# A cheaper VectorE exponential in 96 bursts, the skip product on VectorE, and a second state bank laid out by quarters, in a fused SSM and attention kernel

## The chip, the cores and the metric

One core of one Trainium2 chip. The metric is device time in microseconds (us), the median of several executions. Every experiment ran beside the kernel before on the same chip. Different batches of experiments ran on different chips, so the ratios to the kernel before compare across batches better than the bare times do.

## The reference, cut to what matters

Two branches on one input of 2048 rows and 1024 columns, mixed row by row by a gate.

```python
g = sigmoid((x * gate_w).sum(-1, keepdims=True))
a = A_ref(x, ...)     # SSM: h = Lam_bar*h + Bu over 2048 steps; y = 2*Re(C h) + x*Dskip
b = B_ref(x, ...)     # attention: 32 heads of 32 columns; softmax(q k^T / sqrt(32)) v; then @ wo
return g * a + (1 - g) * b
```

The attention has 32 x 2048 x 2048 exponentials. They decide the time.

## The kernel before

Attention runs as 512 *bursts* in 8 groups of 64 (a group is four heads). A burst makes the scores of four heads, 256 queries and 256 keys in PSUM (the memory that TensorE writes its results to), and two 128x1024 exponentials turn them into bf16 weights. All instruction orders are static. The projections of the next group, the SSM's input products ("u"), its C chains ("c") and the output products fill TensorE's gaps; VectorE evicts them, which means that it copies them out of PSUM, and does the SSM's scans.

In some bursts (the list `DVB`) VectorE does half of one of the two exponentials, so that ScalarE has 512 columns less to do there. VectorE's half needs tiles: two for weights (`xt`), one for bits (`xi`) and one for scratch (`xw`). There are five sets of these, cut from memory that is idle at that time. Sets 0 and 1 lie in the weight buffers of the projections, but their scratch is a separate tile, `Ag[:, 1]`, which both share.

```python
self.xt = half(wx[0]) + half(wx[1]) + half(hx[0]) + half(self.OT[:, 6, :]) + [ub[:, 0], ub[:, 1]]
self.xw = [ag, ag, hx[1][:, 1024:2048].bitcast(F32), self.OT[:, 7, 1024:2048].bitcast(F32), self.ut[:, 1, :]]
# ... cut ...
def x_set(self, B):
    g, pg = divmod(B, 64)
    if g == 7 or B >= 433:
        return 4
    if pg < 52:                      # first 52 bursts of a group: the group's old weight buffer
        return g % 2
    return 2 if g < 4 else 3         # the last 12: other memory, with a scratch of its own

def x_toks(self, k):                 # what a load over set k claims to write
    # ... cut: asserts ...
    return [(n, t0 + t) for n in ("pt", "ptd") for t in range(2)] + [("xi", k), ("xw", max(k, 1))]
```

Every dependency goes through such *tokens*: an operation waits for the last writer of what it reads, and for the last writer and all readers of what it claims to write. `("xw", 1)` stands for the scratch of sets 0 and 1. At burst 58 of a group the weights of the next group but one are loaded over the old buffer. These are three loads of 256 KB on SyncE's queue:

```python
def ld_w(self, g, part, eng="sp"):
    cb = 1024 * part + 128 * g
    self.dma(lambda e: e.dma_start(self.w[:, g % 2, part], self.wsrc[:, :, cb:cb + 128]), [],
             [("w", g % 2, part)] + (self.x_toks(g % 2) if g > 2 else []), "ld_w", eng)
# ... cut ...
            if pg == (58 if g else 24) and g + 2 < GROUPS:
                for part in (1, 2, 0):
                    self.ld_w(g + 2, part)
```

VectorE's half exponential has five steps, dribbled between other VectorE work during the bursts after its own:

```python
self.S.op("dve", ... tensor_scalar(xi, ps[:, 2 * s + 1, :], EXP_A, EXP_B, ALU.mult, ALU.add) ...)          # exp_a, at once
self.dx += [(0.365, ... tensor_scalar(hi, hi, 0.0, 128.0, ALU.max, ALU.mult), [I], [I], "exp_b"),
            (0.603, ... scalar_tensor_tensor(xw, lo, EXP_C2, lo, ALU.add, ALU.mult), [I], [W], "exp_c"),     # W = ("xw", max(k, 1))
            (0.603, ... scalar_tensor_tensor(xw, xw, EXP_C1, lo, ALU.add, ALU.mult), [I, W], [W], "exp_d"),
            (0.603, ... scalar_tensor_tensor(t[:, 1, :], xw, EXP_C0, ev, ALU.add, ALU.mult), [I, W], [("ptd", p)], "exp_f")]
```

## Time and profile before

| | |
|---|---|
| time | 929.05 us (928.53 to 929.23, 4 runs) |
| profiled span, mean granted TensorE clock | 926.5 us, 0.998 |
| bursts with a half exponential on VectorE | 82 |
| ScalarE: spacing of the ends of consecutive operations, median | 0.917 us (1024 columns), 0.490 us (512) |
| ScalarE's floor, 942 x 0.917 + 84 x 0.490 | 905 us |

The spacings come from the trace's records, since durations of overlapping operations say nothing of throughput.

The page of the kernel before (busy time and share; then busy tenths of a fortieth of the span each):

```profile
PE 892.4 (96%) x15095; PEld 525.4 (57%) x15316; DVE 737.3 (80%) x1331; ACT 911.3 (98%) x1034; POOL 8.9 (1%) x39
...
ACT  6999999999999999999999999999999999999997
...
PE 55%; ACT 37%; DVE 5%; issue 1%; SPq 1%; DMA 1%; DVEq 0%
...
L1666 ACT ACTIVATE f_pt<-f_ps 128x1024 bf16<-128x1024 f32 x862 | 814.2, 1209 | 0.6 <-PE f_ps L1650 0.6
```

Windows of the kernel before (busy us and instructions of TensorE, its weight loads, VectorE, ScalarE and GpSimd in this order; then granted clock, DMA share, GB/s):

```profile
200.00:300.00 100.00, 98.10 (x1622) 56.35 (x1643) 89.78 (x159) 100.00 (x114) 0.00 (x0) 1.00 0.22 49
300.00:400.00 100.00, 98.29 (x1702) 58.39 (x1724) 85.26 (x155) 99.96 (x116) 1.41 (x6) 1.00 0.20 46
```

ScalarE is never idle between its start and its end: the large group of exponentials shows 0.6 us of idle time before it in the whole run. TensorE holds more of the chain of waits, but its weight loads (PEld) stand idle for ScalarE's exponentials, so it follows ScalarE, and ScalarE is what bounds. In the list of waits (us in total, times, longest):

```profile
PEld f_ps L1650 <- ACT f_pt L1666: 63.4, 153, 0.6
```

### The profile page before, as it was taken

How to read it: one execution, taken by the hardware profiler on the slowest of the kernel's cores; microseconds unless marked ns; L12 is line 12 of the kernel's file. 1: busy time of each engine (PE TensorE's matmuls, PEld its weight loads, DVE VectorE, ACT ScalarE, POOL GpSimd, SP SyncE). 2: the span in 40 equal slices, each digit the busy share in tenths (PEclk: the TensorE clock that was granted, in tenths of full speed). 3: DMA queues.
4: the chain of work that ended last, by engine and by line, in shares of the span. 5: the costliest groups of instructions: out<-in, count | busy, mean ns of one | idle time of the engine just before them, and what ended most of it. 6: DMA issues, size and time to landing. Idle time of an engine off the chain costs nothing.

```text
span 926.5 us, 33493 instructions
## 1 busy us (share of the span) xinstructions
PE 892.4 (96%) x15095; PEld 525.4 (57%) x15316; DVE 737.3 (80%) x1331; ACT 911.3 (98%) x1034; POOL 8.9 (1%) x39
## 2 busy tenths in 40 slices
PE   8899999999999999999999999999999999999996
PEld 4555755566555655555755755555565655555553
DVE  2799999999888888867889966679888765766775
ACT  6999999999999999999999999999999999999997
POOL 2000000000000000000000000000000000000000
PEclk9999999999999999999999999999999999999999
DMA  9649613210230113113033102133210111434322
GB/s 202 107 79 156 106 31 74 42 42 28 66 72 30 30 43 73 41 40 53 19 75 58 25 16 65 53 66 59 39 38 12 52 52 56 161 88 122 117 65 75
DMA packets 157076, 60.90 MB, mean 66 GB/s; under 512 B 145664, under 2 KB 145664, under 8 KB 156928
## 3 DMA queue, kind: packets, MB, share of 16 engines
q1 hardware_dynamic: 154768, 58.16, 28.3%
q8 instruction: 121, 1.98, 0.9%
q10 hardware_dynamic: 2160, 0.53, 0.3%
q14 instruction: 27, 0.22, 0.1%
HBM read 16.79 MB, written 12.58 MB: 32 GB/s over the span
## 4 chain that ended last, share of the span: by engine, by line
PE 55%; ACT 37%; DVE 5%; issue 1%; SPq 1%; DMA 1%; DVEq 0%
ACT f_pt L1666 33%; PE f_ps L1725 16%; PE f_ps L1650 11%; PE f_ps L1480 8%; PE f_ps L1451 8%; PE f_ps L1421 8%; PE f_ps L1439 4%; SPq L1074 1%; ACT f_ub L1691 1%; ACT f_wb L1691 1%; DVE f_ht L1370 1%; DMA f_xT<-in_A_x_dram 1%; ACT f_Et L1666 1%; ACT f_cT_re L1666 1%; PE f_ps L1486 1%
## 5 line engine op out<-in xcount | busy, mean ns | idle before, releaser
L1666 ACT ACTIVATE f_pt<-f_ps 128x1024 bf16<-128x1024 f32 x862 | 814.2, 1209 | 0.6 <-PE f_ps L1650 0.6
L1725 PEld LDWEIGHTS f_ps<-f_V,f_pt 128*128 128x128 bf16 x6896 | 239.4, 96 | 135.9 <-issue 96.9
L1725 PE MATMUL f_ps<-f_V,f_pt 128*128 128x33 bf16 x6896 | 293.0, 178 | 0.2 <-ACT f_pt L1666 0.2
L1650 PE MATMUL f_ps<-f_Q,f_K 32*128 32x256 bf16 x4096 | 220.9, 273 | 4.2 <-ACT f_pt L1666 1.2
L1650 PEld LDWEIGHTS f_ps<-f_Q,f_K 32*128 32x128 bf16 x4096 | 72.7, 92 | 118.4 <-ACT f_pt L1666 63.4
L1451 PE MATMUL f_ps<-f_xT,f_wb 128*128 128x512 bf16 x448 | 117.4, 377 | 8.2 <-issue 2.1
L1421 PE MATMUL f_ps<-f_xT,f_wb 128*128 128x512 bf16 x406 | 106.7, 378 | 4.5 <-issue 0.5
L1370 DVE TENSOR_TENSOR_SCAN f_ht<-f_pf,f_init,f_ut 128x512 bf16<-128x512 f32 x64 | 80.2, 1271 | 0.0
L1692 DVE TENSOR_SCALAR f_wb<-f_ps 128x512 int32<-128x512 f32 x53 | 36.6, 691 | 52.4 <-PE f_ps L1650 52.3
L1480 PE MATMUL f_ps<-f_cT_im,f_hp 128*128 128x512 bf16 x189 | 71.4, 378 | 3.0
L1511 PE MATMUL f_ps<-f_wb,f_OT 128*128 128x512 bf16 x218 | 57.8, 378 | 3.0 <-issue 0.2
L1451 PEld LDWEIGHTS f_ps<-f_xT,f_wb 128*128 128x128 bf16 x512 | 40.2, 96 | 33.4 <-issue 1.9
L1439 PE MATMUL f_ps<-f_wb,f_xT 128*128 128x128 bf16 x896 | 59.1, 219 | 0.0
L1480 PE MATMUL f_ps<-f_cT_re,f_hp 128*128 128x512 bf16 x147 | 55.5, 378 | 0.2
L1421 PEld LDWEIGHTS f_ps<-f_xT,f_wb 128*128 128x128 bf16 x464 | 36.2, 96 | 28.2 <-DVE f_ub L1457 0.3
L1439 PEld LDWEIGHTS f_ps<-f_wb,f_xT 128*128 128x128 bf16 x896 | 50.4, 97 | 0.0
L1457 DVE CAST f_ub<-f_ps 128x512 bf16<-128x512 f32 x48 | 33.0, 687 | 14.5 <-PE f_ps L1451 14.1
L1362 DVE TENSOR_TENSOR f_tq<-f_ht,f_Et 128x1024 bf16<-128x1024 bf16 x64 | 42.3, 684 | 0.4
L1362 DVE TENSOR_TENSOR f_ut<-f_tq 128x512 f32<-128x512 bf16 x64 | 42.3, 683 | 0.0
L1691 ACT ACTIVATE f_wb<-f_ps 128x512 bf16<-128x512 f32 x53 | 38.4, 725 | 0.1
L1701 DVE SCALAR_TENSOR_TENSOR f_wb<-f_Ag,f_wb 128x512 bf16<-128x512 f32 x53 | 36.5, 689 | 1.2
L1700 DVE SCALAR_TENSOR_TENSOR f_Ag<-f_Ag,f_wb 128x512 f32<-128x512 f32 x53 | 36.3, 685 | 0.7
(160 smaller groups left out, 925.4 us busy)
## 6 DMA issues: line engine op xcount, KB each, us to landing
ag_scratch<-f_Ag SPq DMA_DIRECT2D x32, 256.0 KB, 2.3
f_hp<-ag_scratch SPq DMA_DIRECT2D x32, 256.0 KB, 3.0
f_wb<-in_B_wqkv_dram SPq DMA_DIRECT2D x21, 256.0 KB, 3.5
out_dram<-f_xT SPq DMA_DIRECT2D x16, 256.0 KB, 2.1
f_wb<-in_B_wo_dram SPq DMA_DIRECT2D x1, 1024.0 KB, 6.2
f_OT<-f_On SPq DMA_TRANSPOSE x63, 2.4
f_wb<-in_B_wo_dram SPq DMA_DIRECT2D x1, 768.0 KB
f_wb<-in_B_wqkv_dram ACTq DMA_DIRECT2D x2, 256.0 KB, 4.1
```

The costliest lines, as they stand in the source:

```text
L1362: ops.append((c, lambda: dve(lambda e: e.tensor_tensor(o, a, b, op), r, w() if callable(w) else w)))
L1370: ops.append((1.192, lambda ri=ri: dve(lambda e: e.tensor_tensor_scan(ht[:, ri, :], rr, ut[:, ri, :], self.init[:, ri, j:j + 1], ALU.mult, ...
L1421: mms.append((1, lambda e, f, l, a=a: e.matmul(ps[:, bank, :], w[:, g % 2, part, a, :], xT[:, a, 512 * ch:512 * (ch + 1)], start=f, stop=l ...
L1439: m = e.matmul(ps[:, bank, 128 * q:128 * (q + 1)], xT[:, a, 128 * kt:128 * (kt + 1)], w[:, g % 2, 2, a, :], start=(a == 0), stop=(a == 7))
L1451: mms.append((1, lambda e, f, l, a=a: e.matmul(ps[:, 7, :], bT[:, n % 2, ri, a, :], xT[:, a, 512 * ch:512 * (ch + 1)], start=f, stop=l), [ ...
L1480: mms.append((1, lambda e, f, l, j=j, ri=ri: e.matmul(ps[:, 7, :], hp[:, ri, j, cols], cT[ri][:, j, 512 * cb:512 * (cb + 1)], start=f, sto ...
L1511: mms.append((1, lambda e, f, l, j=j: e.matmul(ps[:, 7, :], OT[:, j, 256 * qb + 128 * r:256 * qb + 128 * (r + 1)], wo[j][0][:, 512 * cb:51 ...
L1650: m = e.matmul(ps[:, 2 * sl[z] + h % 2, 256 * kl:256 * (kl + 1)], K[32 * h:32 * h + 32, g % 2, 128 * kt:128 * (kt + 1)], Q[32 * h:32 * h + ...
L1666: self.act(lambda e: e.activation(self.tile[p], ps[:, 2 * s:2 * s + 2, :], ACT.Exp, scale=SCALE), [("S", s)], [("pt", p)], "exp")
L1691: self.S.op("act", lambda e: e.activation(t[:, 0, :], ps[:, 2 * s, :], ACT.Exp, scale=SCALE), reads=[("S", s)], writes=[("pt", p)], deps=d ...
L1692: self.S.op("dve", lambda e: e.tensor_scalar(xi, ps[:, 2 * s + 1, :], EXP_A, EXP_B, ALU.mult, ALU.add), reads=[("S", s)], writes=[("xi", k ...
L1725: m = e.matmul(ps[:, 6, o:o + 33], self.tile[p][:, h2, 256 * kl + 128 * qt:256 * kl + 128 * (qt + 1)], V[:, g % 2, 2 * i + kl, h, :], star ...
```

## The change

Four intents:
- a four-step exponential on VectorE that leaves bf16 bits (Q scaled at its eviction, bias and scale in ScalarE's exponential);
- 96 bursts in place of 82;
- the product x * Dskip no longer as 128 diagonal matmuls in the C chains, but as 64 VectorE operations on x in rows, loaded by 64 small DMAs;
- the second bank of SSM states laid out by row quarters, so that it is freed quarter by quarter and its C chains can run late.

Sets 2 and 3 of the tiles go, since C chains now use that memory for longer. The lists `ORDER` and `DVB_RUNS` are new. The diff, cut to its core:

```diff
-        self.xw = [ag, ag, hx[1][:, 1024:2048].bitcast(F32), self.OT[:, 7, 1024:2048].bitcast(F32), self.ut[:, 1, :]]
+        self.xw = [ag, ag, self.ut[:, 1, :]]
 ... cut ...
+    def x_group(self, B):
+        g, pg = divmod(B, 64)
+        return g if pg < 54 else g + 1
+
     def x_set(self, B):
-        g, pg = divmod(B, 64)
-        if g == 7 or B >= 433:
-            return 4
-        if pg < 52:
-            return g % 2
-        return 2 if g < 4 else 3
+        return 2 if B >= 433 else self.x_group(B) % 2
 ... cut: exponential ...
-            self.act(... ACT.Exp, scale=SCALE) ...
+            self.act(... ACT.Exp, bias=OCTAVES * LN2, scale=LN2 / 128) ...
+        self.S.op("dve", ... tensor_scalar(xi, ps[:, 2 * s + 1, :], BITS_0, BITS_MIN, ALU.add, ALU.max) ... "exp_a")
+        self.dx += [(0.603, ... scalar_tensor_tensor(xw, lo, 65536.0, lo, ALU.subtract, ALU.mult), [I], [W], "exp_b"),
+                    (0.603, ... scalar_tensor_tensor(xw, lo, CUBE_C, xw, ALU.add, ALU.mult), [I, W], [W], "exp_c"),
+                    (0.603, ... scalar_tensor_tensor(bits, xw, CUBE_K, xi, ALU.mult, ALU.add), [I, W], [("ptd", p)], "exp_d"),
 ... cut: C chain ...
-        for q in range(4):
-            dt = 4 * cb + q
-            mms.insert(5 * q + 3, (0, ... matmul(... xT[:, dt, ...], self.diagD[:, dt, :], start=False, stop=False) ...))
+    def skip_ops(self, ch, tq, cb):          # two operations of 128x256 per C chain
+        ... scalar_tensor_tensor(self.Ag[:, 0, 256 * k:256 * (k + 1)], self.xn[k], self.gcol[:, 0, tt:tt + 1], self.drow[:, c0:c0 + 256], ALU.mult, ALU.mult) ...
         def evac():
+            self.dve(... scalar_tensor_tensor(a, ps[:, 7, :], self.gcol[:, 0, tt:tt + 1], a, ALU.mult, ALU.add) ... "evac_c")
             self.dma(lambda e: e.dma_start(self.agd[tile], a), ... "st_a")
+            if self.c_next < 32:
+                self.ld_xn(*self.c_list[self.c_next])     # two loads of x for the next chain, 64 KB each
```

More of the change, by code (lines that the diff above doesn't have):

```diff
@@ L24 @@
 G_MIN = 1e-30
-RC_MIN = 1e-10
-RC_MAX = 1e12
 class Op:
@@ L930 @@
 ACT_1 = 0.49
-ACT_LAG = 0.466
+ACT_LAG = 0.12
 QK_LAG = 0.449
@@ L938 @@
 DEP = 0.122
-EXP_A = 16713.9646930418
-EXP_B = 4936176.0
-EXP_C2 = 189883.03836007958
-EXP_C1 = 38303098318.667244
-EXP_C0 = 3607248267949745.0
+LOG2E = 1.4426950408889634
+Q_SCALE = 128.0 * LOG2E * SCALE
+OCTAVES = 65
+BITS_0 = 128.0 * (127 + OCTAVES)
+BITS_MIN = 16384.0
+CUBE_C = 3.891446932518378 * 65536.0
+CUBE_K = 0.07826797 * 128.0 / 65536.0 ** 3
+LN2 = 0.6931471805599453
+DEN_MIN = 1e-12 * 2.0 ** OCTAVES
+DEN_MAX = 1e10 * 2.0 ** OCTAVES
 ORDER = "".join(w[0] * int(w[1:]) for w in (
-    "u2 p2 u4 p1 u2 p2 u2 p9 u8 p1 u1 p1 u1 p1 u1 p1 u1 p1 u1 p1 u1 p1 c1 p2 c1 p2 c1 p1 u4 c1 u2 p1 c1 p2 c1 u2 p4 c1 p2 c1 u2 p3 u2 c2 u1 c6 u1 p12 u4 "
-    "p1 u2 p1 u4 p9 c5 p1 c3 u4 p1 u2 p1 u2 p1 u4 p1 u2 p8 u2 p9 c8 p3 o36 ").split())
-DVB_RUNS = ((109, 113), (129, 177), (185, 257), (277, 277), (285, 329), (345, 345), (365, 381), (389, 453), (461, 505))
+    "u2 p3 u1 p3 u1 p1 u4 p2 u2 p5 u3 p2 u2 p2 u1 p3 u1 p3 u1 p1 u5 p1 u1 c3 p8 u2 p2 c1 u3 c1 p1 u1 c1 u2 p1 c2 u2 p2 u2 p2 c2 p1 u2 p4 u2 p2 u2 c1 p1 c1 "
+    "u2 c1 p3 u2 p4 u2 p1 c2 p1 c1 p2 c2 p1 c3 p3 c3 u4 p2 u2 p1 u2 p1 u2 p2 u1 p3 u3 p3 u1 p2 u1 p4 c8 p3 o36 ").split())
+DVB_RUNS = ((65, 65), (70, 70), (73, 73), (84, 84), (114, 118), (121, 121), (129, 129), (134, 134), (137, 141), (150, 162), (165, 177), (182, 202), (205, 209), (214, 238), (241, 241), (246, 246), (249, 257), (262, 262), (265, 265), (270, 278), (281, 281), (286, 294), (297, 309), (314, 326), (329, 333), (340, 340), (346, 346), (358, 370), (373, 373), (381, 381), (386, 394), (402, 402), (405, 413), (418, 418), (421, 421), (426, 434), (437, 441), (446, 450), (453, 453), (459, 459), (462, 462), (465, 465), (470, 486), (489, 493), (498, 498), (501, 501), (508, 508))
 DVB = {B for lo, hi in DVB_RUNS for B in range(lo, hi + 1, 4)}
@@ L991, in __init__ @@
         self.Et = T("Et", [128, 2, 8, 512], BF)
-        hp = T("hp", [128, 2, 8, 512], BF)
-        self.hpb = [hp, self.OT[:, 4:8, :].rearrange("p (r a) n -> p r (a n)", r=2).rearrange("p r (j t) -> p r j t", j=8)]
+        hp = self.hp = T("hp", [128, 2, 8, 512], BF)
+        cols = self.OT[:, 4:8, :].rearrange("p q (r j t) -> p q r j t", r=2, j=8)
+        self.hp_out = [lambda r, j: hp[:, r, j, :].rearrange("p (q t) -> p q t", q=4), lambda r, j: cols[:, :, r, j, :]]
+        self.hp_in = [lambda q, r, j: hp[:, r, j, 128 * q:128 * (q + 1)], lambda q, r, j: cols[:, q, r, j, :]]
         self.hp_of = [0, 1, 0, 0]
@@ L1007, in __init__ @@
         self.ones = T("ones", [128, 128], BF)
-        self.diagD = T("diagD", [128, 8, 128], BF)
+        self.drow = T("drow", [128, 1024], BF)
+        xa = T("xa", [128, 256], BF)
         self.init = T("init", [128, 2, 8], F32)
@@ L1015, in __init__ @@
         self.badb = T("badb", [128, 2], BF)
+        self.xn = [xa[:], self.pf[:, 24:40, :].bitcast(BF).rearrange("p a b -> p (a b)")]
         otf = self.OT.bitcast(F32)
@@ L1030, in __init__ @@
         half = lambda ap: [pair(ap[:, 0:1024]), pair(ap[:, 1024:2048])]
-        hx = [hp[:, r, 4:8, :].rearrange("p a n -> p (a n)") for r in range(2)]
         wx = [self.w[:, x].rearrange("p q a n -> p (q a n)") for x in range(2)]
         ag = self.Ag[:, 1, :]
-        self.xt = half(wx[0]) + half(wx[1]) + half(hx[0]) + half(self.OT[:, 6, :]) + [ub[:, 0], ub[:, 1]]
-        self.xi = [wx[0][:, 2048:3072], wx[1][:, 2048:3072], hx[1][:, 0:1024], self.OT[:, 7, 0:1024], self.ut[:, 0, :]]
-        self.xi = [ap.bitcast(I32) for ap in self.xi]
-        self.xw = [ag, ag, hx[1][:, 1024:2048].bitcast(F32), self.OT[:, 7, 1024:2048].bitcast(F32), self.ut[:, 1, :]]
+        self.xt = half(wx[0]) + half(wx[1]) + [ub[:, 0], ub[:, 1]]
+        self.xi = [wx[0][:, 2048:3072], wx[1][:, 2048:3072], self.ut[:, 0, :]]
+        self.xi = [ap.bitcast(F32) for ap in self.xi]
+        self.xw = [ag, ag, self.ut[:, 1, :]]
         self.tile += self.xt
@@ L1096, in begin @@
         pool, dve, act = self.pool, self.dve, self.act
-        warm = self.hpb[0][:, 0, 0, :]
+        warm = self.hp[:, 0, 0, :]
         dve(lambda e: e.memset(warm, 0.0), [], ["warm"])
@@ L1165, in evac @@
             kw.update(dict(writes=[tok]) if first else dict(acc=[tok]))
-            if eng is dve:
+            if tok[0] == "K":
                 S.op("dve", lambda e: e.tensor_copy(dst, src), name="evac_qk", **kw)
+            elif eng is dve:
+                S.op("dve", lambda e: e.tensor_scalar(dst, src, Q_SCALE, None, ALU.mult), name="evac_qk", **kw)
             else:
-                S.op("act", lambda e: e.activation(dst, src, ACT.Copy), name="evac_qk", **kw)
+                S.op("act", lambda e: e.activation(dst, src, ACT.Copy, scale=Q_SCALE), name="evac_qk", **kw)
         for word in self.OPENING.split():
@@ L1222, in opening @@
                 self.nmath = len(self.bg2)
-                self.diag_d()
     def spare(self, us):
@@ L1308, in math, with ld_d, ld_xn @@
         return ops
-    def diag_d(self):
-        for j in range(8):
-            self.pool(lambda e, j=j: e.tensor_scalar(self.diagD[:, j, :], self.ident[:], self.pf[:, 3, j:j + 1], 0.0, ALU.mult, ALU.add),
-                      ["ident", ("pf", 3)], [("diagD", j)])
+    def ld_d(self):
+        self.dma(lambda e: e.dma_start(self.drow[:], self.d["A_Dskip"].partition_broadcast(128)), [], ["drow"], "ld_d")
+    def ld_xn(self, ch, tq, cb):
+        tt = 4 * ch + tq
+        for k in range(2):
+            over = ["iot", "ioth", "ioti", ("pw2", 0), ("pw2", 1)] if k and self.c_next == 0 else []
+            c0 = 512 * cb + 256 * k
+            self.dma(lambda e, k=k, c0=c0: e.dma_start(self.xn[k], self.x2[128 * tt:128 * (tt + 1), c0:c0 + 256]), [], [("xn", k)] + over, "ld_xn")
+        self.c_next += 1
+    def skip_ops(self, ch, tq, cb):
+        tt = 4 * ch + tq
+        ops = []
+        for k in range(2):
+            c0 = 512 * cb + 256 * k
+            ops.append((0.335, lambda k=k, c0=c0: self.dve(lambda e: e.scalar_tensor_tensor(self.Ag[:, 0, 256 * k:256 * (k + 1)], self.xn[k], self.gcol[:, 0, tt:tt + 1],
+                                                                                            self.drow[:, c0:c0 + 256], ALU.mult, ALU.mult),
+                                                           [("xn", k), "drow", "g0"], [("Ag", 0)] if k == 0 else [("Ag", 0, 1)], "skip")))
+        return ops
     def fold_ops(self, j):
@@ L1352, in item_ops @@
         b = self.hp_of[ch]
-        hp = self.hpb[b]
-        er, ei = self.Et[:, 0, j, :], self.Et[:, 1, j, :]
+        hp = self.hp_out[b]
         k = self.ub_of(n)
@@ L1358, in item_ops @@
         t = [tq[:, i, :] for i in range(4)]
+        t4 = [tq[:, i, :].rearrange("p (q t) -> p q t", q=4) for i in range(4)]
         ops = []
@@ L1376, in item_ops @@
         hw = ["warm"] if ch == 0 and j == 0 else []
-        late = lambda: []
-        if ch == 2 and j >= 4:
-            late = lambda: self.x_toks(2)
         if b == 1 and j == 0:
             hw = ["fX", "fY", "m_c"] + self.EFtok + ["gp%d" % i for i in range(4)]
-        tt(0.335, hp[:, 0, j, :], t[0], t[1], ALU.subtract, [("tq", 0)], lambda: [("hp", b, j, 0)] + hw + late())
-        tt(0.335, hp[:, 1, j, :], t[2], t[3], ALU.add, [("tq", 2)], lambda: [("hp", b, j, 1)] + hw + late())
+        tt(0.335, hp(0, j), t4[0], t4[1], ALU.subtract, [("tq", 0)], lambda: self.hp_toks(b, j, 0) + hw)
+        tt(0.335, hp(1, j), t4[2], t4[3], ALU.add, [("tq", 2)], lambda: self.hp_toks(b, j, 1) + hw)
         if j == 7 and ch < 3:
@@ L1386, in item_ops, with hp_toks, hp_all @@
         return ops
+    def hp_toks(self, b, j, ri):
+        return [("hp", b, j, ri, q) for q in range(4 if b else 1)]
+    def hp_all(self, b, qs=range(4)):
+        return [("hp", b, j, ri, q) for j in range(8) for ri in range(2) for q in (qs if b else (0,))]
     def carry(self):
@@ L1425, in d_qk @@
             dst, tok = self.Q[:, z, :], ("Q", z)
+            evac = lambda: self.dve(lambda e: e.tensor_scalar(dst, ps[:, bank, :], Q_SCALE, None, ALU.mult), [("bank", bank)], [tok], "evac_qk")
         else:
             dst, tok = self.K[:, g % 2, 512 * ch:512 * (ch + 1)], ("K", g % 2, ch)
-        return self.chain(mms, "proj", lambda: self.dve(lambda e: e.tensor_copy(dst, ps[:, bank, :]), [("bank", bank)], [tok], "evac_qk"), bank)
+            evac = lambda: self.dve(lambda e: e.tensor_copy(dst, ps[:, bank, :]), [("bank", bank)], [tok], "evac_qk")
+        return self.chain(mms, "proj", evac, bank)
     def d_v(self, g, f, bank=7):
@@ L1473, in d_c @@
         b = self.hp_of[ch]
-        hp = self.hpb[b]
+        hp = self.hp_in[b]
         tt = 4 * ch + tq
-        cols = slice(128 * tq, 128 * (tq + 1))
         mms = []
@@ L1479, in d_c @@
             for ri in range(2):
-                mms.append((1, lambda e, f, l, j=j, ri=ri: e.matmul(ps[:, 7, :], hp[:, ri, j, cols], cT[ri][:, j, 512 * cb:512 * (cb + 1)], start=f, stop=l),
-                            [("hp", b, j, ri), ("cTf", ri, j)]))
-        for q in range(4):
-            dt = 4 * cb + q
-            mms.insert(5 * q + 3, (0, lambda e, f, l, q=q, dt=dt: e.matmul(ps[:, 7, 128 * q:128 * (q + 1)], xT[:, dt, 128 * tt:128 * (tt + 1)], self.diagD[:, dt, :],
-                                                                          start=False, stop=False), [("diagD", dt)] + self.xtok(ch)))
+                mms.append((1, lambda e, f, l, j=j, ri=ri: e.matmul(ps[:, 7, :], hp(tq, ri, j), cT[ri][:, j, 512 * cb:512 * (cb + 1)], start=f, stop=l),
+                            [("hp", b, j, ri, tq if b else 0), ("cTf", ri, j)]))
         a = self.Ag[:, 0, :]
@@ L1492, in evac @@
         def evac():
-            self.dve(lambda e: e.tensor_scalar(a, ps[:, 7, :], self.gcol[:, 0, tt:tt + 1], None, ALU.mult), [("bank", 7), "g0"], [at], "evac_c")
-            self.dma(lambda e: e.dma_start(self.agd[tile], a), [at], [("agd", tile)], "st_a")
+            self.dve(lambda e: e.scalar_tensor_tensor(a, ps[:, 7, :], self.gcol[:, 0, tt:tt + 1], a, ALU.mult, ALU.add), [("bank", 7), "g0", ("Ag", 0, 1)], [at], "evac_c")
+            self.dma(lambda e: e.dma_start(self.agd[tile], a), [at, ("Ag", 0, 1)], [("agd", tile)], "st_a")
+            if self.c_next < 32:
+                self.ld_xn(*self.c_list[self.c_next])
             self.c_left[ch] -= 1
@@ L1501, in ld_a @@
         tile = self.a_order[k]
-        x = [("hp", 0, j, ri) for j in range(8) for ri in range(2)] if k == 0 else []
+        x = self.hp_all(0) if k == 0 else []
         self.dma(lambda e: e.dma_start(self.Al[k % 8], self.agd[tile]), [("agd", tile)], [("Al", k % 8)] + x, "ld_a")
@@ L1554, in plan @@
                 late = B in DVB and q == 1
-                parts.append((B + 2 + (2 if late else 0), B, q))
+                parts.append((max(B + 2, min(B + 4, NBURST - 1)) if late else B + 2, B, q))
         todo = [sorted(parts[32 * U:32 * U + 32]) for U in range(NBURST // BURSTS)]
@@ L1614, in split_pv @@
         return need + rest[:len(rest) - n], rest[len(rest) - n:]
+    def x_group(self, B):
+        g, pg = divmod(B, 64)
+        return g if pg < 54 else g + 1
     def x_set(self, B):
-        g, pg = divmod(B, 64)
-        if g == 7 or B >= 433:
-            return 4
-        if pg < 52:
-            return g % 2
-        return 2 if g < 4 else 3
+        return 2 if B >= 433 else self.x_group(B) % 2
     def x_of(self, B, n):
-        return len(self.tile) - 10 + 2 * self.x_set(B) + n
+        return len(self.tile) - 6 + 2 * self.x_set(B) + n
     def x_toks(self, k):
-        t0 = len(self.tile) - 10 + 2 * k
+        t0 = len(self.tile) - 6 + 2 * k
         assert not any(self.left_in.get(t0 + t, 0) for t in range(2)), (self.p, k)
@@ L1665, in exp @@
         else:
-            self.act(lambda e: e.activation(self.tile[p], ps[:, 2 * s:2 * s + 2, :], ACT.Exp, scale=SCALE), [("S", s)], [("pt", p)], "exp")
+            self.act(lambda e: e.activation(self.tile[p], ps[:, 2 * s:2 * s + 2, :], ACT.Exp, bias=OCTAVES * LN2, scale=LN2 / 128), [("S", s)], [("pt", p)], "exp")
     def dve_exp(self, B, s, p):
@@ L1671, in dve_exp @@
         xi, xw, t = self.xi[k], self.xw[k], self.tile[p]
-        halves = xi.bitcast(U16).rearrange("p (n two) -> p n two", two=2)
-        lo, hi = halves[:, :, 0], xi.bitcast(I16).rearrange("p (n two) -> p n two", two=2)[:, :, 1]
-        ev = xi.bitcast(BF).rearrange("p (n two) -> p n two", two=2)[:, :, 1]
+        lo = xi.bitcast(U16).rearrange("p (n two) -> p n two", two=2)[:, :, 0]
+        bits = t[:, 1, :].bitcast(I16)
         deps = []
-        use = (k, B // 64 if k < 2 else 0)
+        wg = self.x_group(B)
+        use = (k, wg if k < 2 else 0)
         self.x_now = k
@@ L1680, in dve_exp @@
             if k < 2:
-                assert self.busy_w != B // 64
+                assert self.busy_w != wg and not self.proj[wg]
                 over = [("w", k, q) for q in range(3)] + [("Ag", 1)]
-            elif k < 4:
-                assert self.c_left[k - 2] == 0
-                over = [("hp", k - 2, j, ri) for j in range(8) for ri in range(2)]
             else:
@@ L1690, in dve_exp @@
                 deps += [self.S.tok_w.get(o)] + self.S.tok_r.get(o, [])
-        self.S.op("act", lambda e: e.activation(t[:, 0, :], ps[:, 2 * s, :], ACT.Exp, scale=SCALE), reads=[("S", s)], writes=[("pt", p)], deps=deps, name="exp")
-        self.S.op("dve", lambda e: e.tensor_scalar(xi, ps[:, 2 * s + 1, :], EXP_A, EXP_B, ALU.mult, ALU.add), reads=[("S", s)], writes=[("xi", k)], deps=deps, name="exp_a")
+        self.flush_dx()
+        self.S.op("act", lambda e: e.activation(t[:, 0, :], ps[:, 2 * s, :], ACT.Exp, bias=OCTAVES * LN2, scale=LN2 / 128), reads=[("S", s)], writes=[("pt", p)], deps=deps, name="exp")
@@ L1693, in dve_exp @@
+        self.S.op("dve", lambda e: e.tensor_scalar(xi, ps[:, 2 * s + 1, :], BITS_0, BITS_MIN, ALU.add, ALU.max), reads=[("S", s)], writes=[("xi", k)], deps=deps, name="exp_a")
         kw = max(k, 1)
         I, W = ("xi", k), ("xw", kw)
-        assert not self.dx, (self.p, [c for c, _ in self.dx], self.log[-8:])
         self.waiting.add(B)
         self.last_dx, self.dx_due = True, B + 3
-        self.dx += [(0.365, lambda: self.dve(lambda e: e.tensor_scalar(hi, hi, 0.0, 128.0, ALU.max, ALU.mult), [I], [I], "exp_b")),
-                    (0.603, lambda: self.dve(lambda e: e.scalar_tensor_tensor(xw, lo, EXP_C2, lo, ALU.add, ALU.mult), [I], [W], "exp_c")),
-                    (0.603, lambda: self.dve(lambda e: e.scalar_tensor_tensor(xw, xw, EXP_C1, lo, ALU.add, ALU.mult), [I, W], [W], "exp_d")),
-                    (0.603, lambda: self.dve(lambda e: e.scalar_tensor_tensor(t[:, 1, :], xw, EXP_C0, ev, ALU.add, ALU.mult), [I, W], [("ptd", p)], "exp_f")),
-                    (0.0, lambda: self.waiting.discard(B))]
+        self.dx += [(0.603, lambda: self.dve(lambda e: e.scalar_tensor_tensor(xw, lo, 65536.0, lo, ALU.subtract, ALU.mult), [I], [W], "exp_b")),
+                    (0.603, lambda: self.dve(lambda e: e.scalar_tensor_tensor(xw, lo, CUBE_C, xw, ALU.add, ALU.mult), [I, W], [W], "exp_c")),
+                    (0.603, lambda: self.dve(lambda e: e.scalar_tensor_tensor(bits, xw, CUBE_K, xi, ALU.mult, ALU.add), [I, W], [("ptd", p)], "exp_d")),
+                    (0.0, lambda: self.done_dx(B))]
@@ new lines, in done_dx, with flush_dx, dx_ready @@
+    def done_dx(self, B):
+        self.waiting.discard(B)
+        self.dx_end[B] = self.dve_t
+    def flush_dx(self):
+        while self.dx:
+            c, f = self.dx.pop(0)
+            self.dve_t += c + DEP * (c > 0)
+            f()
+    def dx_ready(self, quarters):
+        todo = [B for B, q in quarters if B in DVB and q == 1]
+        if any(B in self.waiting for B in todo):
+            self.flush_dx()
+        return max([self.dx_end.get(B, 0) + 0.12 for B in todo], default=0.0)
@@ L1740, in normalize @@
                                                   accum_out=self.osum[:, U:U + 1]), ["O", ("rc", U)], [("On", U % 2), ("os", U)], "norm")
-        x = [("hp", 1, j, ri) for j in range(8) for ri in range(2)] if g >= 4 and qb == 0 else []
-        assert not x or self.c_left[1] == 0
+        x = self.hp_all(1, [g - 4]) if g >= 4 and qb == 0 else []
+        assert not x or self.c_left[1] <= 14 - 2 * g
         if g < 4 and qb == 0:
@@ L1747, in normalize @@
                 x += [("ub", k, ri) for k in (2, 3) for ri in range(2)]
-        if qb == 0 and g >= 6:
-            assert all(self.x_set(B) != 3 or B < U * BURSTS for B in DVB)
-            x += self.x_toks(3)
         self.dma(lambda e: e.dma_start_transpose(self.OT[:, g, 256 * qb:256 * (qb + 1)].rearrange("p (t q) -> p t q", t=2),
@@ L1785, in build @@
         proj[0] = [self.d_qk(0, 0, 2), self.d_qk(0, 0, 3)]
+        self.proj = proj
         us, cs = [], []
+        self.c_list, self.c_next, self.bgx = [], 0, []
         for ch in range(4):
@@ L1790, in build @@
                     us.append((ch, 8 * ch + j, ri, self.d_u(j, ch, 8 * ch + j, ri)))
-            for cb in range(2):
-                for tq in range(4):
+            for tq in range(4):
+                for cb in range(2):
                     cs.append((ch, self.d_c(ch, tq, cb, len(cs))))
+                    cs[-1][1].pre = lambda ch=ch, tq=tq, cb=cb: self.skip_ops(ch, tq, cb)
+                    self.c_list.append((ch, tq, cb))
         self.c_left = [8, 8, 8, 8]
@@ L1816, in build @@
         log = self.log = []
+        self.dx_end = {}
         for p in range(first, NBURST):
@@ L1828, in build @@
                 self.dve_t = max(self.dve_t, T + QK_LAG) + 0.608
-                ta = max(ta, self.dve_t + 0.19)
+                ta = max(ta, self.dve_t + 0.1)
             nq += len(self.quarters[p])
@@ L1835, in build @@
             head, tail = self.split_pv(p, ntail)
+            rdy = self.dx_ready(head)
             self.pv(head)
             second()
-            pe = T + QK_PE + PV_PE * len(head)
+            pe = max(T + QK_PE + PV_PE * len(head), rdy + PV_PE)
             if ends:
@@ L1852, in build @@
                 self.later.pop(0)[1]()
+            if not self.c_next and len(self.tabled) == 8:
+                self.ld_d()
+                self.ld_xn(*self.c_list[0])
             if pg == (58 if g else 24) and g + 2 < GROUPS:
@@ L1883, in build @@
                     kind = order[0]
+                    assert kind != "c" or not self.bgx
                     if kind == "p":
@@ L1897, in build, with take @@
                         ok = self.items_done >= 8 * (cs[0][0] + 1) and p > self.item_p + 1 and len(self.folded) == 8
-                        take = lambda: cs.pop(0)[1]
+                        def take():
+                            self.bgx, self.bgx_at = cs[0][1].pre(), p + 2
+                            return cs.pop(0)[1]
                     else:
@@ L1915, in build @@
                     quota += 1
+            rdy = self.dx_ready(tail)
             self.pv(tail)
             ready = pe + 0.2
+            pe = max(pe, rdy)
             tp = pe + PV_PE * len(tail) + 0.1
@@ L1931, in build @@
             if ended is not None:
+                while self.bgx:
+                    c, f = self.bgx.pop(0)
+                    f()
+                    self.dve_t += c
                 ended.evac()
@@ L1960, in sources @@
         out = []
-        for src in (self.bg, self.bg2):
-            if not src:
+        for src in (self.bgx, self.bg, self.bg2):
+            if not src or src is self.bgx and self.p < self.bgx_at:
                 continue
@@ L1979, in tail @@
         z = self.ut[:, 1, 0:65]
-        dve(lambda e: e.memset(z, 0.0), [], ["z"] + [("ut", r) for r in range(2)] + self.x_toks(4))
-        assert not self.dx, (self.p, [c for c, _ in self.dx], self.log[-8:])
+        dve(lambda e: e.memset(z, 0.0), [], ["z"] + [("ut", r) for r in range(2)] + self.x_toks(2))
         def check(u0, u1, s0, s1, c):
@@ L1987, in check @@
             rcs, oss = [("rc", u) for u in range(u0, u1)], [("os", u) for u in range(s0, s1)]
-            dve(lambda e: e.tensor_scalar(t, ra, RC_MAX, None, ALU.is_le), rcs, [("ut", 0)])
-            dve(lambda e: e.scalar_tensor_tensor(t, ra, RC_MIN, t, ALU.is_ge, ALU.mult, accum_out=chk[:, c:c + 1]), rcs + [("ut", 0)], [("ut", 0), ("chk", c)])
+            dve(lambda e: e.tensor_scalar(t, ra, 1.0 / DEN_MIN, None, ALU.is_le), rcs, [("ut", 0)])
+            dve(lambda e: e.scalar_tensor_tensor(t, ra, 1.0 / DEN_MAX, t, ALU.is_ge, ALU.mult, accum_out=chk[:, c:c + 1]), rcs + [("ut", 0)], [("ut", 0), ("chk", c)])
             dve(lambda e: e.scalar_tensor_tensor(z2, osum[:, s0:s1], 0.0, z[:, s0:s1], ALU.mult, ALU.is_equal, accum_out=chk[:, c + 1:c + 2]), oss + ["z"], ["z2", ("chk", c + 1)])
@@ L1996, in preload @@
                          reads=["ident", ("hi", 2 * r), ("lo", 2 * r)], name="preload", writes=[("tb", 2 + r)] + ([("S", 1)] if r == n == 0 else []), **({} if r == n == 0 else dict(acc=[("S", 1)])))
+        self.dx_ready([(NBURST - 2, 1), (NBURST - 1, 1)])
         check(0, 63, 0, 63, 0)
```

## The prediction

> **What bounds it now.** ScalarE. The page has it busy 98% of 926.5 us, the windows view 99.96 to 100 us of every 100 from 100 to 800 us. Its operations overlap, so I took the spacing of their ends in the trace: 0.917 us (median) for a 128x1024 exponential, 0.490 us for a 128x512 one. There are 942 of the first and 84 of the second (82 bursts give half of one exponential to VectorE): a floor of 942 x 0.917 + 84 x 0.49 = 905 us. By the timeline the first exponential starts at 9.7 us and the last ends at 918.0: 908.3 us, about 4 over the floor; then 8.5 us of tail. TensorE (96% busy) holds most of the chain of waits (55%, ScalarE 37%), but its weight loads wait some 75 us for exponentials (waits), so it follows ScalarE. VectorE is 80% busy, 94 to 96% from 50 to 200 us.
>
> **What the change does.**
> - ScalarE: the diff's lists hold 82 bursts before and 96 after. 14 more exponentials are halved: 14 x (0.917 - 0.490) = 6.0 us off the engine that bounds. The new bias should cost nothing: the Trainium skill ("ScalarE: Activation LUTs", "What ACT_TABLE_LOAD costs") gives 186 ns + 0.833 ns per element with immediate scale and bias, 93 ns more for a pointer operand. The trace agrees with the immediate form: shortest durations 1017 and 597 ns at 1024 and 512 elements.
> - VectorE: a burst's exponential goes from five operations (0.69 + 0.45 + 3 x 0.69 = 3.2 us by the groups) to four (2.75 us): 82 x 3.2 = 262 us becomes 96 x 2.75 = 264 us. The skip product adds 64 operations of 128x256 at some 0.4 us (an estimate from the 0.42 us of other 128x256 operations): +26 us. The eviction stays 0.75 us. VectorE's busy time rises from 737 to about 765 us, still below the 94 to 96% that the early stretches bear without costing ScalarE anything.
> - TensorE: 128 diagonal matmuls of 128x128 go; their busy 27.9 us overlaps, some 7 us of real time (estimate: a quarter of the 0.22 us pitch of 512-column matmuls each). Off the critical path; slack for the C chains.
> - Moves: C chains later, bursts spread more evenly (some from burst 65 on, more from 256 to 288), 64 small loads of x. Queue room is ample (mean 66 GB/s).
>
> **On the critical path:** the 6.0 us only; the rest makes room for it. I expect the excess over the floor to stay at 4 to 5 us. The profile's span should go from 926.5 to about 921.
>
> **Predicted: 923.5 us, 920.5 to 927.5 (8 in 10).** Faster by over 2%: 0.01; within 2%: 0.96; slower by over 2%: 0.03.
>
> **What would show it.** Right: ScalarE still at 99 to 100 us per 100; 928 full exponentials 0.917 us apart, 98 half ones, floor 899 us; VectorE 755 to 775 us busy; no diagonal matmuls; TensorE's share unchanged or a point down; head and tail unchanged. Wrong: gaps between exponentials behind a late first step of VectorE's exponential (QK weight loads waiting for VectorE), above all before 300 us.
>
> **What would make it wrong.** A bias taken from memory (93 ns on 1024 operations, up to +95 us); VectorE behind its static order, so that score banks come free late; x loads or the skip product holding the C chain's eviction; a strided read or int16 write slower than 0.69 us; or the guard choosing the fallback.

## More of the kernel before

The timeline of SyncE's queue (SPq) around the weight loads of one group:

```profile
234.90 7.42 SPq L1079 DMA_DIRECT2D f_wb<-in_B_wqkv_dram  x3
242.37 1.54 SPq L1494 DMA_DIRECT2D ag_scratch<-f_Ag  x1
```

The three loads hold the queue for 7.4 us, because each claims what the one before it claimed and so waits for it to land. The store of a C chain's result comes behind them. Nothing here needs either soon: ScalarE shows no gap in this stretch, so it costs nothing.

## The result, and the profile after

The changed kernel takes 977.71 us (976.15 to 978.73, 4 runs) against 929.05 us: ratio 1.0523, interval [1.0505, 1.0541]. The output is correct.

The page of the changed kernel:

```profile
PE 892.3 (92%) x14969; PEld 517.4 (53%) x15188; DVE 758.7 (78%) x1369; ACT 905.3 (93%) x1034; POOL 6.5 (1%) x31
...
ACT  6999999997799986999959999599998999999997
...
PEclk9999999999899997999979999799998999999999
...
PE 44%; ACT 43%; DMA 6%; DVE 4%; issue 2%; SPq 1%; DVEq 0%
...
L1691 ACT ACTIVATE f_pt<-f_ps 128x1024 bf16<-128x1024 f32 x848 | 802.1, 1136 | 40.5 <-PE f_ps L1675 40.2
...
L1720 DVE SCALAR_TENSOR_TENSOR f_Ag<-f_wb 128x512 f32<-128x512 uint16 x77 | 52.7, 684 | 47.2 <-DMA f_wb<-in_B_wqkv_dram 47.1
```

Windows of the changed kernel:

```profile
200.00:300.00 100.00, 87.34 (x1476) 51.17 (x1496) 82.40 (x139) 88.80 (x101) 0.00 (x0) 0.95 0.22 47
300.00:400.00 100.00, 85.94 (x1362) 45.88 (x1383) 79.95 (x147) 86.41 (x101) 1.48 (x6) 0.93 0.29 60
```

ScalarE's work is as predicted: 928 and 98 operations, their ends 0.917 and 0.490 us apart in the median. But its row has holes. The spacings of its ends show seven gaps of over 0.5 us beyond these figures (not counting the run's first and last microseconds): 11.2, 12.8, 0.7, 12.7, 11.8, 3.8 and 0.9 us, 53.9 us in all. That is all of the difference to the predicted span: 974.4 - 921 = 53.4 us.

The last line of the page's extract names the cause: the second step of VectorE's exponential (`exp_b`, L1720) stood 47.1 us waiting for loads of attention weights. In the list of waits of the changed kernel that is five times:

```profile
DVE f_Ag L1720 <- DMA f_wb<-in_B_wqkv_dram: 47.1, 5, 12.1
...
ACT f_pt L1691 <- PE f_ps L1675: 40.2, 7, 12.7
...
PE f_ps L1509 <- DVE f_Ag L1518: 22.2, 3, 11.2
```

The first stall in the timeline of the changed kernel, in order of time:

```profile
230.53 0.69 DVE L1715 TENSOR_SCALAR f_wb<-f_ps 128x512 f32<-128x512 f32 x1 [0.47 <-PE f_ps L1675]
...
234.07 0.38 PE L1509 MATMUL f_ps<-f_cT_im,f_hp 128*128 128x512 bf16 x1
234.29 0.38 PE L1509 MATMUL f_ps<-f_cT_re,f_hp 128*128 128x512 bf16 x1
...
234.44 6.34 SPq L1085 DMA_DIRECT2D f_wb<-in_B_wqkv_dram  x3
...
243.33 0.69 DVE L1720 SCALAR_TENSOR_TENSOR f_Ag<-f_wb 128x512 f32<-128x512 uint16 x1 [10.25 <-DMA f_wb<-in_B_wqkv_dram]
...
246.74 0.63 PE L1509 MATMUL f_ps<-f_cT_im,f_hp 128*128 128x512 bf16 x1 [10.70 <-DVE f_Ag L1518]
...
247.17 0.63 PE L1509 MATMUL f_ps<-f_cT_re,f_hp 128*128 128x512 bf16 x1
...
248.81 1.94 ACT L1691 ACTIVATE f_pt<-f_ps 128x1024 bf16<-128x1024 f32 x2 [11.06 <-PE f_ps L1675]
```

Burst 121 (burst 57 of its group, counted from 0) does its first step at 230.5. The weight loads are issued at 234.4 and land one after the other until about 243.3. Only then does the second step run, although it writes `Ag` and the loads write `wb`. (The `wb` that it reads is another buffer: the profile leaves buffer numbers out, and by the code burst 121 has set 0 while the loads go to set 1.) Nothing else runs on VectorE in these 10 us. Its order is fixed: all 1369 operations follow each other in the same order here and in e1 below, where the stall is gone. So no eviction comes, TensorE waits, and then ScalarE.

TensorE's clock is an effect. Before the stall 512-column matmuls start about 0.22 us apart (234.07 to 234.29), just after it 0.43 us (246.74 to 247.17). The Trainium skill ("TensorE: Matmul & The Clock Gate", "Wait — 56ns, not 53.3ns?") gives 215.7 ns warm and 426.7 ns cold for that size, and its section "What's actually happening" halves the clock after an idle window of some 3.4 us. The trace agrees, these matmuls following an idle stretch of 10.7 us; and where the stalls are gone (e4, e8 below) the mean clock is back at 0.998.

### The profile page after: what moved, and what is told of

Read it like the earlier page. It is cut to its first block, busy times and chain, and to the rows that moved or that the text cites. A ratio compares the mean times of both kernels' runs of the same rounds, so it can differ in the third digit from the quotient of the medians. Undisturbed runs are those within 1.5% of the kernel's fastest.

```text
span 974.4 us, 33369 instructions
## 1 busy us (share of the span) xinstructions
PE 892.3 (92%) x14969; PEld 517.4 (53%) x15188; DVE 758.7 (78%) x1369; ACT 905.3 (93%) x1034; POOL 6.5 (1%) x31
## 4 chain that ended last, share of the span: by engine, by line
PE 44%; ACT 43%; DMA 6%; DVE 4%; issue 2%; SPq 1%; DVEq 0%
ACT f_pt L1691 38%; PE f_ps L1763 12%; PE f_ps L1675 9%; PE f_ps L1481 7%; PE f_ps L1449 6%; PE f_ps L1509 5%; DMA f_wb<-in_B_wqkv_dram 5%; PE f_ps L1469 3%; ACT f_wb L1714 2%; ACT f_ub L1714 1%; SPq L1080 1%; DMA f_xT<-in_A_x_dram 1%; ACT f_Et L1691 1%; ACT f_cT_re L1691 1%; SPq L1786 1%
## 5 line engine op out<-in xcount | busy, mean ns | idle before, releaser
L1691 ACT ACTIVATE f_pt<-f_ps 128x1024 bf16<-128x1024 f32 x848 | 802.1, 1136 | 40.5 <-PE f_ps L1675 40.2
L1763 PEld LDWEIGHTS f_ps<-f_V,f_pt 128*128 128x128 bf16 x6784 | 235.4, 96 | 138.2 <-issue 88.9
L1763 PE MATMUL f_ps<-f_V,f_pt 128*128 128x33 bf16 x6784 | 288.7, 178 | 0.3
L1481 PE MATMUL f_ps<-f_xT,f_wb 128*128 128x512 bf16 x449 | 119.0, 381 | 18.8 <-DVE f_Ag L1518 12.5
L1449 PE MATMUL f_ps<-f_xT,f_wb 128*128 128x512 bf16 x406 | 108.5, 384 | 7.4 <-DVE f_ub L1487 3.4
L1720 DVE SCALAR_TENSOR_TENSOR f_Ag<-f_wb 128x512 f32<-128x512 uint16 x77 | 52.7, 684 | 47.2 <-DMA f_wb<-in_B_wqkv_dram 47.1
L1715 DVE TENSOR_SCALAR f_wb<-f_ps 128x512 f32<-128x512 f32 x77 | 52.8, 686 | 27.3 <-PE f_ps L1675 26.6
L1714 ACT ACTIVATE f_wb<-f_ps 128x512 bf16<-128x512 f32 x77 | 53.5, 695 | 14.3 <-PE f_ps L1675 14.2
L1481 PEld LDWEIGHTS f_ps<-f_xT,f_wb 128*128 128x128 bf16 x512 | 40.5, 96 | 45.4 <-DVE f_Ag L1518 12.5
L1509 PE MATMUL f_ps<-f_cT_re,f_hp 128*128 128x512 bf16 x153 | 58.8, 384 | 0.6
L1722 DVE SCALAR_TENSOR_TENSOR f_wb<-f_Ag,f_wb 128x512 int16<-128x512 f32 x77 | 52.7, 685 | 0.7
L1721 DVE SCALAR_TENSOR_TENSOR f_Ag<-f_wb,f_Ag 128x512 f32<-128x512 uint16 x77 | 52.7, 685 | 0.6
L1487 DVE CAST f_ub<-f_ps 128x512 bf16<-128x512 f32 x48 | 33.1, 689 | 12.7 <-PE f_ps L1481 11.7
```

Source lines behind the costliest of these rows:

```text
L1449: mms.append((1, lambda e, f, l, a=a: e.matmul(ps[:, bank, :], w[:, g % 2, part, a, :], xT[:, a, 512 * ch:512 * (ch + 1)], start=f, stop=l ...
L1481: mms.append((1, lambda e, f, l, a=a: e.matmul(ps[:, 7, :], bT[:, n % 2, ri, a, :], xT[:, a, 512 * ch:512 * (ch + 1)], start=f, stop=l), [ ...
L1509: mms.append((1, lambda e, f, l, j=j, ri=ri: e.matmul(ps[:, 7, :], hp(tq, ri, j), cT[ri][:, j, 512 * cb:512 * (cb + 1)], start=f, stop=l), ...
L1691: self.act(lambda e: e.activation(self.tile[p], ps[:, 2 * s:2 * s + 2, :], ACT.Exp, bias=OCTAVES * LN2, scale=LN2 / 128), [("S", s)], [("p ...
L1714: self.S.op("act", lambda e: e.activation(t[:, 0, :], ps[:, 2 * s, :], ACT.Exp, bias=OCTAVES * LN2, scale=LN2 / 128), reads=[("S", s)], wr ...
L1715: self.S.op("dve", lambda e: e.tensor_scalar(xi, ps[:, 2 * s + 1, :], BITS_0, BITS_MIN, ALU.add, ALU.max), reads=[("S", s)], writes=[("xi" ...
```

## The experiments

My theory after reading the traces: a **false dependency**. The weight loads claim `("xw", 1)` although they never write the scratch `Ag[:, 1]`. Before, bursts 52 to 63 of a group had other sets with other scratch tokens, so nobody asked for that token near the loads. Now every burst up to 432 uses it, and the dribbled steps of a burst at 57 or 58 land just behind the loads (in four of the five stalls; the fifth and smallest, 2.9 us, is burst 381, the 61st of its group). Rivals: the clock fell by itself; VectorE is overfull; the new exponential or the skip product are to blame.

All outputs are right. "Gaps" are ScalarE's end spacings beyond 0.917 or 0.490 us, summed where over 0.5 us.

| run | time, us | ratio to before | clock | VectorE waits for weight loads, us | gaps, us |
|---|---|---|---|---|---|
| the change | 977.71 | 1.0523 | 0.971 | 47.1 (5) | 53.9 |
| e1 no false token | 934.01 | 1.0063 | 0.992 | 0 | 11.7 |
| e2 loads side by side | 957.07 | 1.0316 | 0.982 | 29.3 (4) | 34.7 |
| e3 before, token added | 972.86 | 1.0477 | 0.978 | 39.7 (4) | 44.3 |
| e4 e1 and e2 | 925.20 | 0.9968 | 0.998 | 0 | 2.7 |
| e5 e1, skip on TensorE | 930.17 | 1.0023 | 0.996 | 0 | 5.5 |
| e6 e4 with 82 bursts | 929.99 | 1.0012 | 0.996 | 0 | 1.3 |
| e7 before, four steps | 928.80 | 1.0001 | 0.997 | 0 | 0 |
| e8 e1, loads on GpSimd's queue | 923.15 | 0.9942 | 0.998 | 0 | 0 |
| e9 e8, skip on TensorE | 924.92 | 0.9959 | 0.997 | 0 | 0 |

The kernel before had a median of 928.18 us beside e1 to e3, 928.51 beside e4 to e7 and 928.59 beside e8 and e9.

### e1: the token taken away

```diff
-        return [(n, t0 + t) for n in ("pt", "ptd") for t in range(2)] + [("xi", k), ("xw", max(k, 1))]
+        return [(n, t0 + t) for n in ("pt", "ptd") for t in range(2)] + [("xi", k)] + ([("xw", 2)] if k == 2 else [])
```

> The changed kernel with one token taken out: the weight loads no longer claim the scratch tile of VectorE's exponential, which they do not write (same instructions in the same order on every engine, fewer waits). Theory (false dependency): the five idle stretches of VectorE before the exponential's second step, 47.1 us in all, vanish with the 53 us of ScalarE gaps behind them; clock back to 0.99 or more, about 923 us (920 to 926). Rival 1 (the tensor clock fell by itself, 0.971): clock and time stay at about 977. Rival 2 (96 bursts and the skip product overfill VectorE): the waits move to other VectorE operations and the time stays over 940.

The five waits and their gaps are gone, the clock is back at 0.992, and the time fell by 43.7 us, with the same instructions in the same order on every engine. So the token explains most, and the clock and an overfull VectorE are out as the main cause. But 934.0 is not the expected 923, and still 0.6% slower than before: two gaps of 5.4 us and one of 0.9 us are left. The timeline of e1 around the second:

```profile
573.88 6.38 SPq L1085 DMA_DIRECT2D f_wb<-in_B_wqkv_dram  x3
580.30 0.58 SPq L1519 DMA_DIRECT2D ag_scratch<-f_Ag  x1
580.93 0.43 SPq L1326 DMA_DIRECT2D f_xa<-in_A_x_dram  x1
...
583.99 0.48 DVE L1335 SCALAR_TENSOR_TENSOR f_Ag<-f_xa,f_gcol,f_drow 128x256 f32<-128x256 bf16 x1 [4.53 <-DMA f_xa<-in_A_x_dram]
...
589.25 1.94 ACT L1691 ACTIVATE f_pt<-f_ps 128x1024 bf16<-128x1024 f32 x2 [5.29 <-PE f_ps L1675]
```

The three weight loads hold SyncE's queue for 6.4 us. Behind them stand a C chain's store and the small load of x that VectorE's next skip product needs. VectorE waits 4.5 us for it, and ScalarE misses 5.3 us. That is a second form of the same coupling: now the *position in the queue*, not the token, ties VectorE to the weight loads.

### e2: the three loads side by side

```diff
... cut: the old load, which claims every token ...
+        deps, w = [], [("w", g % 2, part)]
+        if g > 2:
+            toks = self.x_toks(g % 2)
+            if part == 1:
+                self.ld_deps = [o for t in toks for o in [self.S.tok_w.get(t)] + self.S.tok_r.get(t, [])]
+            deps = self.ld_deps
+            w += toks if part == 0 else []
... cut: the load, issued with these deps and w ...
```

> The changed kernel, false token kept, but the three weight loads of a group wait only for the earlier readers of the tiles, no longer for each other. Theory: the stall is the time of three loads one after the other (about 9 us from the first issue to the last landing); side by side they land in 4 to 5 us, so each of the four big stalls falls from 10 to 12 us to 4 to 7 us and the time from 977 to 950 to 958 us. Rival (the serial order of the loads does not matter, the wait is for something else): still about 977.

957.1 us, inside the expected range. In the list of waits of e2:

```profile
DVE f_Ag L1727 <- DMA f_wb<-in_B_wqkv_dram: 29.3, 4, 7.9
```

The waits of VectorE are 29.3 us in four (7.9 us at most, a little over what I expected), where the change has 47.1 us in five. So their serial order made up a good third of the stall.

### e3: the token given to the kernel before

```diff
-        ... + [("xi", k), ("xw", max(k, 1))]
+        ... + [("xi", k), ("xw", max(k, 1))] + ([("xw", 2), ("xw", 3)] if k < 2 else [])
```

> The kernel before, same instructions and order, with only the token added: its weight loads also claim the scratch tiles of its sets 2 and 3. Theory: the four bursts 189, 253, 317 and 381, whose exponentials start three bursts (about 5 us) after the loads are issued, now wait for the last of three serial loads: four stalls of 3 to 6 us, time 929 to 937-950 us. If the false token is harmless by itself and the damage came from the new exponential or the skip product: stays within 931.

972.9 us: the kernel before, with nothing of the change and not one instruction moved, loses almost as much as the change does. The token alone is enough. I had the size wrong. In the list of waits of e3:

```profile
DVE f_OT L1699 <- DMA f_wb<-in_B_wqkv_dram: 20.6, 2, 10.4
...
DVE f_hp L1699 <- DMA f_wb<-in_B_wqkv_dram: 19.1, 2, 10.0
```

Four waits of about 10 us, not 3 to 6. I had looked for the first burst that *starts* after the loads. The timeline shows that the burst before it stalls. First `exp_a` (L1692) and `exp_c` (L1699) of that burst in the kernel before, then in e3:

```profile
344.82 0.68 DVE L1692 TENSOR_SCALAR f_hp<-f_ps 128x512 int32<-128x512 f32 x1
...
348.01 0.68 DVE L1699 SCALAR_TENSOR_TENSOR f_hp<-f_hp 128x512 f32<-128x512 uint16 x1
```

```profile
344.50 0.68 DVE L1692 TENSOR_SCALAR f_hp<-f_ps 128x512 int32<-128x512 f32 x1
...
356.98 0.69 DVE L1699 SCALAR_TENSOR_TENSOR f_hp<-f_hp 128x512 f32<-128x512 uint16 x1 [9.19 <-DMA f_wb<-in_B_wqkv_dram]
```

The step comes 12.5 us after `exp_a` where it came 3.2 us after it, because it stands in the program behind the point at which the loads claim the token.

### e4: both mended

The edits of e1 and e2 together.

> The changed kernel without the false token (as e1) and with the three weight loads side by side (as e2). Theory: what e1 lost (934 instead of 923 us) are two gaps of 5.4 us on ScalarE behind skip products that waited 4.3 and 4.5 us for a small load of x; that load stood on the in-order SyncE queue behind three weight loads of which each waited for the last one's landing (queue held 6.4 us). Side by side the queue is held for 2 us or less, the gaps go, and ScalarE is back at its floor: 921 to 925 us, 0.5 to 0.8% faster than before. Rival (96 bursts plus the skip product are simply too much for VectorE at these two places): still 930 or more, the gaps at 250 and 589 us remain.

925.2 us, 0.3% faster than before. This is 0.2 us above the expected range: two gaps of 1.2 and 1.5 us remain at the same two places, for the queue is still held for about 2 us.

### e5: no small loads, serial order kept

As e1, with the diagonal matmuls back inside the C chains' pieces and no skip operations and no loads of x.

> As e1 (no false token, weight loads still one after the other), but the skip product back on TensorE as 128 diagonal matmuls inside the same pieces, no skip operations on VectorE and no loads of x; all else in the same order. Theory: without small x loads nothing that VectorE needs stands behind the weight loads, so the two gaps of 5.4 us go although the loads stay serial: 921 to 926 us; the skip product off TensorE is by itself worth under 2 us. Rival (serial weight loads hurt by themselves, or the removal of the diagonal matmuls carries the gain): 930 or more.

930.2 us: neither story in full. The 4.5 us waits for x are gone, but gaps of 1.9 and 3.5 us remain at the same places. The list of waits of e5 says why:

```profile
DVE f_Ag L1525 <- DMA ag_scratch<-f_Ag: 5.9, 2, 3.2
```

The eviction of a C chain waits for the *store* of the chain before, which reads the same tile and also stands behind the weight loads. So the queue's order is to blame and not the x loads as such; my expectation had overlooked the store.

### e8 and e9: the loads on another queue

e8 is e1 (false token gone, serial order kept) with the weight loads issued from GpSimd's queue, on a semaphore of their own (the edits for these two are cut here):

```diff
-                    self.ld_w(g + 2, part)
+                    self.ld_w(g + 2, part, "pool")
```

> As e1 (no false token, the three weight loads of a group one after the other), but those loads issued from GpSimd's queue, which is otherwise nearly empty. Theory: what e1 lost against e4 and what e4 still loses (two gaps of 1.1 and 1.4 us) is SyncE's in-order queue being held by the weight loads; on another queue the serial order harms nobody: 920 to 924 us, no VectorE wait for x loads over 2 us, gaps at 246 to 250 and 581 to 589 us gone. Rival (the traffic of the loads or their serial order itself delays the small loads): 928 us or more, VectorE still waiting 4 us for them.

923.15 us (922.71 to 924.41, 5 runs), ratio 0.9942, interval [0.9929, 0.9956]. No gap over 0.5 us is left. The timeline of e8 at the second of the two places:

```profile
575.68 0.48 DVE L1335 SCALAR_TENSOR_TENSOR f_Ag<-f_xa,f_gcol,f_drow 128x256 f32<-128x256 bf16 x1 [0.43 <-DMA f_xa<-in_A_x_dram]
576.08 0.68 DVE L1720 SCALAR_TENSOR_TENSOR f_Ag<-f_wb 128x512 f32<-128x512 uint16 x1
```

The skip product waits 0.4 us where it waited 4.5, though the weight loads move the same bytes in the same serial order. This beats both kernels. One side effect of the edit is not separated: the DMAs left on SyncE take turns on their semaphores in another rotation. But e4, which keeps the semaphores and only shortens the hold to 2 us, points the same way. A window of e8 (TensorE, its weight loads, VectorE, ScalarE and GpSimd in this order):

```profile
200.00:300.00 100.00, 99.26 (x1675) 56.89 (x1674) 93.24 (x158) 99.73 (x114) 2.67 (x3) 1.00 0.25 54
```

The same stretch of the change had ScalarE at 88.8 us and the clock at 0.95. The page of e8:

```profile
PE 904.1 (98%) x15188; PEld 515.8 (56%) x15188; DVE 758.4 (82%) x1369; ACT 904.7 (98%) x1034; POOL 22.6 (2%) x49
```

e9 is e8 with the skip product back on TensorE, so it measures that move alone.

> As e8, with the skip product back on TensorE (128 diagonal matmuls, no skip operations, no x loads). With the queue out of the way this measures the move of the skip product alone. Theory (TensorE and VectorE both have slack, ScalarE bounds): within 1 us of e8. Rival (the lighter C chains carry part of the gain): 2 us or more slower than e8; (VectorE's 64 added operations cost): 2 us or more faster.

924.9 us, 1.8 us slower than e8, between my 1 us and the rival's 2 us. Every run of e9 (924.43 to 925.75 us) is slower than every run of e8 (922.71 to 924.41 us), on the same chip beside the same runs of the kernel before, so a small difference is there. ScalarE has no gap over 0.5 us in either, but the mean spacings of its ends are 0.9225 and 0.511 us in e9, 0.9217 and 0.500 us in e8: over 928 and 98 operations that is about 1.8 us of many small delays. So moving the skip product is worth some 2 us here. Whether the 128 matmuls fewer on TensorE give it, the runs do not show.

### e6 and e7: the expected gain, part by part

e6 is e4 with 14 bursts of the list given back to ScalarE.

> As e4 with 14 of the 96 bursts (spread over the list) given back to ScalarE: 82 as in the kernel before. Theory (ScalarE bounds, each burst is worth 0.917 - 0.490 = 0.43 us): 6.0 us slower than e4, about 929 us, the same as before. Rival (the gain of e4 comes from the lighter C chains or the cheaper exponential): within 2 us of e4.

930.0 us, 4.8 us slower than e4 (5.7 us in the profiled spans, 928.3 against 922.6, but e4's profiled execution was its fastest), where I expected 6.0. With 82 bursts the mended kernel is no faster than the kernel before, so the 14 bursts carry the gain of e4.

e7 is the kernel before with the four-step exponential alone.

> The kernel before with only its VectorE exponential changed: four operations that leave bf16 bits, Q scaled at eviction, bias and scale in ScalarE's exponential; 82 bursts, sets and skip product as before. Theory: ScalarE keeps its 905 us floor, the bias costs nothing, so 927 to 930 us; VectorE's busy time falls by some 35 us (82 x 0.45). Rival (the bias or the strided and int16 accesses cost time): more than 932 us, or exponentials over 0.92 us apart.

928.8 us, ratio 1.0001. The page of e7:

```profile
PE 893.3 (96%) x15095; PEld 525.7 (57%) x15316; DVE 705.9 (76%) x1249; ACT 911.3 (98%) x1034; POOL 9.2 (1%) x39
```

VectorE is busy 705.9 us where it was 737.3, and the time does not move: VectorE does not bound. ScalarE's spacings stay at 0.917 and 0.490 us and its shortest durations at 1017 and 597 ns, so the bias is free.

## Why the prediction was right or wrong

It was wrong: 977.7 us against 923.5.

**The step that failed** is the one under "On the critical path": "the 6.0 us only; the rest makes room for it", with "the excess over the floor" staying "at 4 to 5 us". The excess grew by 53.9 us of gaps. Two things are behind it, both shown:
- *The token* (e1: 43.7 us less without it; e3: 44.7 us more with it in the kernel before, 972.86 - 928.18). The prediction's list of moves does not mention that sets 2 and 3 go, and so does not ask what their separate scratch tokens had kept apart.
- *The queue* (e8 against e1: 10.9 us). "Queue room is ample (mean 66 GB/s)" is a statement about bytes. The bytes were never the matter. The queue was held by loads that waited for each other, and the change put something urgent behind them. In the changed kernel itself this loss is hidden behind the token's stalls (VectorE waits at most 1.9 us for a load of x there); it shows once the token is gone.

The list of what would make it wrong came near in "VectorE behind its static order" and "x loads ... holding the C chain's eviction", but it named neither a shared token nor a held queue, and I gave a slowdown of over 2% a chance of 3%. Its sign for being wrong, a late *first* step "above all before 300 us", missed too: in the stall shown above the first step came in time and the *second* was late, and the gaps lie between 250 and 748 us, only one of them before 300.

**What was right**, in the changed kernel or once the two couplings were gone:
- ScalarE bounds, and its operations cost what I said: 928 at 0.917 us and 98 at 0.490 us, floor 899 us; e8 has a span of 921.0 us, predicted "about 921", and a time of 923.15 us, predicted 923.5.
- VectorE busy 755 to 775 us: 758.7 us. It is fuller in e8 (93 us of 100 in the window shown) and delays nobody.
- The bias is free, the four steps cost 0.69 us each, and the diagonal matmuls are gone.
- 14 bursts were put at 6.0 us and are worth 4.8 (medians) to 5.7 us (spans).

That e8 comes within 0.4 us of the predicted time is partly luck. e8 gains 5.4 us on the kernel before (928.59 - 923.15), but e9, which has the 96 bursts without the move of the skip product, gains only 3.7 (928.59 - 924.92). The prediction gave that move no worth of its own.

What stays open: by what way the skip product's move saves its 1.8 us, and whether the quarter layout of the second bank is worth anything by itself. No run took it out.

## What to carry to other kernels

When a change removes a buffer, ask which *waits* the buffer kept apart, not only whether its memory is free: follow each dependency that the survivors now share to its other claimants, loads above all. A dependency that is false, or a queue that is held, can cost nothing for as long as nobody asks for it at that moment, so look in the trace of before for long holds (here 7.4 us on SyncE's queue) and ask what the change will put behind them. And where an engine's order is fixed, as VectorE's is here, one late step can cost the whole wait for every engine that it feeds (here a wait of 10.25 us on VectorE became an idle stretch of 11.06 us on ScalarE).

## What the Trainium skill lacked or had wrong

- "DMA: Bandwidth & Descriptors", "Issuing engines are not separate DMA queues": it says that initiating DMAs on several engines will only save the sequencer's time to initiate them, usually small. Here moving 18 weight loads from SyncE to GpSimd, with the same bytes and the same serial order, took 934.0 us to 923.2 (ratios to the kernel before beside them: 1.0063 and 0.9942): here a load that waits for a semaphore held its queue (6.4 us for three loads) and all that stood behind it. The page says elsewhere ("Anatomy of one DMA — SWDGE (gpsimd) path") that the wait is the issuing sequencer's, but not what follows for the choice of queue.
- "ScalarE: Activation LUTs", "What ACT_TABLE_LOAD costs": 186 ns + 0.833 ns per element with an overlap of 93 ns would be 946 and 520 ns from one operation to the next at 1024 and 512 columns (an estimate worked out from the page); here the ends lie 917 and 490 ns apart, 29 to 30 ns less, with PSUM as the source. The passage does not say for which memory its figures hold.
- No page that I read speaks of a scheduler's own false dependencies; here one such token was worth 44 us of 929 (e1 and e3).
